# Windowed attention and a gated feed-forward layer: the last two batches' attention outputs with queries on partitions, turned through DRAM

## The chip, the cores and the metric

The kernel runs on one core of a Trainium2 chip. The metric is the device time of one execution in microseconds; lower is better. A core has a matrix engine (PE), a vector engine (DVE), a scalar engine (ACT), GpSimd (POOL), and a sync engine (SP) whose work here is to issue DMA transfers. SPq stands for the queue of instructions of that sync engine.

## The reference

```python
B, H, S, D = 4, 8, 768, 64           # n_sink = 4, window = 128
scores = q @ k.T / sqrt(D)           # per batch and head
keep = (pos_k < 4) | ((0 <= pos_q - pos_k) & (pos_q - pos_k < 128))
a = exp(scores) where keep, divided by its sum over the keys
x = (a @ v), heads side by side      # (B*S, 512)
out = (relu(x @ w_gate) * (x @ w_val)) @ w_out   # 512 -> 1536 -> 512
```

Each query sees the first four keys and the 128 keys up to its own. The output has 3072 rows of 512 float32 values.

## The kernel before

**Units.** A unit is one pair of heads of one batch: four units a batch (`NP`), 16 in all. Unit u of batch b is number 4b + u. Keys are cut into blocks of 128 columns of `kE`; from the second block on, a block holds the four sink keys and 124 or so keys of the window, so that a query needs two neighbouring blocks only.

**Scores.** `Sg(u, s)` multiplies key blocks (the stationary operand, 64 rows for each head, the two heads in the two row halves of the array) with the queries (the moving operand) into a pair of PSUM banks. ACT takes the exponentials into `ee` (keys on partitions, queries along the columns, in bf16), and DVE multiplies them by a mask. A unit has three score groups, s = 0, 1, 2.

**Values.** `V(u, part)` takes half of the queries (384, `CUT`). `V1` multiplies `ee` by a block of ones, which gives the sums of the exponentials in 64 rows for each head; `V3` multiplies `ee` by the values `vn`. In both, `ones` or `vn` is stationary (64 columns for each head, two heads in the two column halves) and `ee` is moving. `V2` turns the sums, takes reciprocals and turns them back (two 32x32 block transposes by DVE), and `V4` multiplies and writes `xT`, with the features of x on partitions, as the feed-forward layer needs it.

**Feed-forward.** `chunk(b, g, m)` makes 128 of the 1536 hidden features for 384 tokens: four matmuls with `wg`, four with `wv`, a relu by ACT, a product by DVE into `hT`. It reads `xT` of all four units of the batch. `ffn2` is the second matrix product, twelve matmuls for 128 tokens, then a copy by ACT to `ot` and a store by SP.

**The order.** Nothing is reordered by a scheduler: each engine does its instructions in program order. The loop near the end runs over 96 slots, one chunk each: 24 slots a batch, 12 for the first half of the tokens (g = 0), 12 for the second. In a slot come first the things in `prep[s]` (loads, casts, transfers), then the chunk, then what `plan[s]` lists (scores and values of units to come), then three matmuls of `ffn2`. Batch 0 is done ahead of the loop and in its first slots; batch b's attention runs while batch b - 1 is in the feed-forward layer. With a `w` string of pairs, the kernel before puts two items (V or S) into every second slot.

**Keys and queries of batches 2 and 3** (units 8 to 15, `ND` = 8) come another way: `to_dram` (on POOL) writes them in bf16 to DRAM tensors `kd` and `qd`, `turn` (on SP) reads them back with five transposing DMAs, four into `kE` and one into `qT`, and `sinks` copies the four sink columns. When each happens follows from the plan:

```python
t = at["S", i - NP, 2] + 1        # the slot after the last scores of the unit with the same buffers
prep[t - 6].append(("td", i))     # to_dram
prep[t].append(("turn", i))
prep[at["S", i, 0] - 1].append(("sinks", i))
```

The values of a batch are loaded to `vf` by 13 DMAs on SP (`load_v`), seven slots ahead of the first V, and cast to `vn` by POOL in seven blocks (`cast_v`), some three slots ahead.

**Buffers.** Two pairs of PSUM banks `PP` take scores, values and sums in turn; three banks `G` serve the chunks, the fourth `ffn2`. There are two `xT`, two `hT`, two `vn`, four `ee`, four `kE` and `qT`, three `ot`.

Of the kernel before, what the change touches and what calls it, by code (L numbers as in the profile page):

```python
# [9 lines left out]
F32 = mybir.dt.float32  # L10
BF16 = mybir.dt.bfloat16
Alu = mybir.AluOpType
# [7 lines left out]
def kernel(  # L20
# [12 lines left out]
    nc = tc.nc  # L33
    B, H, S, D = q.shape
    assert (B, H, S, D) == (4, 8, 768, 64)
    NP = H // 2
# [14 lines left out]
    kf = [const.tile([128, S], F32, name=f"kf{i}") for i in range(NQ)]  # L51
    qf = [const.tile([128, S], F32, name=f"qf{i}") for i in range(NQ)]
    vf = const.tile([128, 7, H, 64], F32, name="vf")
    vn = [const.tile([128, 7, H, 64], BF16, name=f"vn{i}") for i in range(2)]
    qT = [const.tile([128, S], BF16, name=f"qT{i}") for i in range(NT)]
    kE = [const.tile([128, 896], BF16, name=f"kE{i}") for i in range(NT)]
    ee = [const.tile([128, 3, 2, 512], BF16, name=f"ee{i}") for i in range(NE)]
    qn = [const.tile([128, S], BF16, name=f"qn{i}") for i in range(2)]
    kn = [const.tile([128, S], BF16, name=f"kn{i}") for i in range(2)]
    wg = const.tile([128, KO, d_ff], BF16, name="wg")  # L60
# [27 lines left out]
            [(2, 1, 140, 255, 0), (3, 1, 267, 507, 0)] + VLAST]  # L88
    VSEG0 = [[(0, 0, 0, 247, 0), (1, 0, 247, 499, 120), (2, 1, 0, 140, 244), (3, 1, 140, 152, 372)],
             [(2, 1, 152, 267, 0), (3, 1, 267, 507, 0)] + VLAST]  # L90

    class Unit:
        def __init__(self, i):
# [33 lines left out]
                nc.sync.dma_start(out=vf[a0:a1, j, :, :], in_=v[b, :, s0:s0 + a1 - a0, :].rearrange("h s d -> s h d"))  # L127

    def cast_v(b, j, rows=128, copy=nc.gpsimd.tensor_copy):
        flat = lambda ap: ap.rearrange("p h d -> p (h d)")  # L130
        copy(flat(vn[b % 2][0:rows, j, :, :]), flat(vf[0:rows, j, :, :]))  # L131

    def cast_kq(u):
        for src, dst in ((kf[u.i % NQ], kn[u.i % 2]), (qf[u.i % NQ], qn[u.i % 2])):
# [2 lines left out]
    def gate(u):  # L137
# [4 lines left out]
    ND = 2 * NP  # L142
    kd, qd = ([nc.dram_tensor(f"{x}d{i}", (S, 128), BF16, kind="Internal").ap() for i in range(ND, B * NP)]
              for x in "kq")

    def to_dram(u):
        for x, dst in ((k, kd), (q, qd)):
            nc.gpsimd.dma_start(out=dst[u.i - ND].rearrange("s (h d) -> s h d", h=2),  # L148
                                in_=x[u.b, 2 * u.p:2 * u.p + 2].rearrange("h s d -> s h d"))
# [21 lines left out]
    def setup():  # L171
        nc.vector.memset(warm[:], 0.0)
        nc.scalar.activation(warm[:], warm[:], Act.Exp, bias=0.0, scale=1.0)
        make_identity(nc, ident)

        nc.gpsimd.memset(band[:], 1.0)
        nc.gpsimd.affine_select(out=band[:], in_=band[:], compare_op=Alu.is_ge, fill=0.0, base=0,
                                pattern=[[1, 256]], channel_multiplier=-1)
        nc.gpsimd.affine_select(out=band[:], in_=band[:], compare_op=Alu.is_ge, fill=0.0, base=127,
                                pattern=[[-1, 256]], channel_multiplier=1)  # L180
        nc.gpsimd.affine_select(out=msk[:, 0, 0:247], in_=band[:, 0:247], compare_op=Alu.is_ge, fill=0.0,
                                base=119, pattern=[[0, 247]], channel_multiplier=-1)
        cp, ms = nc.vector.tensor_copy, nc.vector.memset
        for i in range(NT):
            ms(kE[i][:, 120:124], 0.0)
            ms(kE[i][:, 396:508], 0.0)
            ms(kE[i][:, 784:896], 0.0)
        ms(ones[:], 1.0)
        ms(vn[0][:, 3, :, :], 0.0)
        ms(vf[:, 6, :, :], 0.0)  # L190
        cp(msk[:, 0, 247:499], band[:, 4:256])
        ms(msk[0:4, 0, 247:499], 1.0)
        ms(msk[0:4, 0, 0:120], 1.0)
        ms(msk[0:4, 0, 120:247], 0.0)
        bias(mb[:, 0, 0:499], msk[:, 0, 0:499])
        bias(mb[:, 1, 0:140], band[:, 0:140])
        bias(mb[:, 1, 140:152], band[:, 4:16])
        ms(mb[0:4, 1, 140:152], 0.0)
# [16 lines left out]
    def pair():  # L215
        rot[0] += 1
        return PP[rot[0] % 2]
# [76 lines left out]
    def sums(u, part, out, w):  # L294
        segs = (VSEG if u.b else VSEG0)[part]
        for i, (j, g, c0, c1, o0) in enumerate(segs):
            for h in range(2):
                nc.tensor.matmul(out=out[64 * h:64 * h + 64, o0:o0 + c1 - c0], lhsT=w(j, h),  # L298
                                 rhs=ee[u.i % NE][:, g, h, c0:c1], start=i == 0, stop=i == len(segs) - 1,
                                 skip_group_check=True)  # L300
# [7 lines left out]
    def V2(u, part, pv, pd):  # L308

        t1 = npool.tile([128, CUT], F32, name="t1")  # L310
        R = npool.tile([128, CUT], F32, name="R")
        r = npool.tile([128, CUT // 32], F32, name="r")
        nc.vector.transpose(out=t1[:], in_=pd[:, 0:CUT])  # L313
        nc.vector.reciprocal(r[:], t1[:].rearrange("p (c e) -> p c e", e=32)[:, :, 0])
        nc.vector.transpose(out=R[:].rearrange("p (c e) -> p c e", e=32),  # L315
                            in_=r[:].unsqueeze(2).to_broadcast([128, CUT // 32, 32]))
        return u, part, pv, R

    def V3(u, part, pv):
        sums(u, part, pv, lambda j, h: vn[u.b % 2][:, j, 2 * u.p + h, :])  # L320

    def V4(u, part, pv, R):
        nc.vector.tensor_tensor(xT[u.b % 2][:, u.p, CUT * part:CUT * part + CUT], pv[:, 0:CUT], R[:], op=Alu.mult)  # L323
        ready[u.b, u.p, part] = True

    def V(u, part):
        x = V1(u, part)
        V3(*x[:3])
        V4(*V2(*x))

    gvn = [0]

# [34 lines left out]
    with tc.manual_schedule():  # L367
# [65 lines left out]
        def put(s, y, n):  # L433
            st = (y[0], n * NP + int(y[1]), int(y[2]) if len(y) > 2 else 0)
            at[st] = s
            plan[s].append(st)
# [5 lines left out]
        for s, w in {12: "T0", 13: "T1", 14: "S00 S01", 15: "S10 S11", 16: "T2", 17: "S20 S21", 18: "V00",  # L442
                     19: "V10 T3", 20: "V20", 21: "S30 S31", 22: "V30 S02"}.items():
            for y in w.split():
                put(s, y, 1)
        for b in range(2, B + 1):
            if b < B:
                w = ("Vp01 Sp12 Vp11 Sp22 Vp21 Sp32 Vp31 Sn00 Sn01 Sn10 "
                     "Vn00 Sn11 Sn20 Vn10 Sn21 Sn30 Vn20 Sn31 Vn30 Sn02")
            else:  # L450
                w = "Vp01 Sp12 Vp11 Sp22 Vp21 Sp32 Vp31"
            for x, y in enumerate(w.split()):
                put(24 * (b - 1) + x // 2 * 2, y[0] + y[2:], b - (y[1] == "p"))
        prep = [[] for _ in slots]
        prep[1] += [("half", 6), ("half", 7), ("v", 0, 3), ("v", 0, 4), ("w", 6, 8), ("v", 0, 5), ("v", 0, 6),
                    ("w", 8, 10), ("w", 10, 12)]
# [1 line left out]
        prep[10] += [("kq", 4), ("load", 7), ("kq", 5)]  # L458
        prep[13] += [("kq", 6)]
        prep[15] += [("v", 1, j) for j in range(7)]  # L460
        prep[16] += [("kq", 7), ("td", 8), ("wo",)]
        for i in range(ND, len(U)):
            t = at["S", i - NP, 2] + 1
            if i > ND:
                prep[t - 6].append(("td", i))
            prep[t].append(("turn", i))
            prep[at["S", i, 0] - 1].append(("sinks", i))
            assert t < at["S", i, 0] - 2
        for b in range(2, B):
            s0 = at["V", b * NP, 0]  # L470
            prep[s0 - 7].append(("lv", b))
            for j in range(7):
                prep[s0 - 3 + j // 2 if j < 6 else s0].append(("v", b, j))

        f2 = deque()
        for s, (b, g, m) in enumerate(slots):
            for x in prep[s]:
                if x[0] == "kq":
                    cast_kq(U[x[1]])
                elif x[0] == "load":  # L480
                    gate(U[x[1]])
                    load_kq(U[x[1]])
                elif x[0] == "half":
                    cast_half(x[1])
                elif x[0] == "w":
                    load_w(*x[1:])
                elif x[0] == "wo":
                    for c in range(3):
                        load_wo(c)
                elif x[0] == "td":  # L490
                    to_dram(U[x[1]])
                elif x[0] == "turn":
                    turn(U[x[1]])
                elif x[0] == "sinks":
                    sinks(U[x[1]], nc.gpsimd.tensor_copy)
                elif x[0] == "lv":
                    for j in range(7):
                        load_v(x[1], j)
                else:
                    cast_v(*x[1:])  # L500
            chunk(b, g, m)
            for what, i, x in plan[s]:
                if what == "T":
                    T(U[i])
                elif what == "H":
                    T_half(NP + i)
                elif what == "S":
                    Sg(U[i], x)
                else:
                    V(U[i], x)  # L510
            for _ in range(3):
                if f2:
                    f2.popleft()()
            if s == 23:
                f2 += [lambda t=t, mm=mm: ffn2(0, t, mm) for t in range(6) for mm in range(FM)]
            if b > 0 and m == FM - 1:
                f2 += [lambda b=b, t=t, mm=mm: ffn2(b, t, mm) for t in range(3 * g, 3 * g + 3) for mm in range(FM)]
# [38 lines left out]
```

The softmax here doesn't subtract the row's maximum and nothing guards it: scores larger than these inputs give would overflow.

## Time and profile before

| what | value |
|---|---|
| time, median of 3 runs | 263.45 us (263.05 to 265.11) |
| span of the profiled execution | 261.9 us |
| PE busy | 247.7 us, 95% of the span |
| DVE, ACT, POOL busy | 151.2, 116.5, 73.0 us |
| share of the 16 DMA engines, hardware queue of SP | 34.3% |
| start of slots 24, 34 and 48 (first chunk matmul, L340) | 75.12, 100.29 and 133.43 us |
| start of the last slot, 95 | 240.34 us |
| chain of waits, the largest shares | L360 20%, L340 19%, L345 19%, L298 (pp) 7% |

In the profile, L340 and L345 are the first product of the feed-forward layer, L360 the second, L282 the scores, L298 the sums and values (`ones` and `vn`), L286 the exponentials, L289 the masks, L313 to L323 the normalization, L154 and L155 the transposing DMAs of `turn`, L127 the loads of v, L148 the transfers of `to_dram`, L131 the casts of v. A row of the timeline has the start and duration in microseconds, the engine, the line, the operation, the result and operands with their form, the number of instructions merged into the row, and in brackets what the engine waited for. A form such as 128\*64 says how many rows and columns of the PE array an instruction uses.

### The profile page before, as it was taken

The numbers are of one execution on the slowest core, as the hardware profiler recorded it, in microseconds if no ns is written. First come the engines' busy times: TensorE is split into PE (matmuls) and PEld (weight loads), VectorE is DVE, ScalarE is ACT, GpSimd is POOL, SyncE is SP. The second block draws the span as 40 slices with busy tenths as digits, with TensorE's granted clock in tenths as the row PEclk, the third lists the DMA queues.
The fourth block names the chain that finished last, engine by engine and source line by source line (L and its number), as shares of the span: only waits on it lengthen the run. The fifth ranks groups of instructions, "written<-read, shape, count | busy, mean of one in ns | idle before, by whom it ended". The sixth has DMA issues, their size and how long they took to land.

```text
span 261.9 us, 5490 instructions
## 1 busy us (share of the span) xinstructions
PE 247.7 (95%) x2143; PEld 140.5 (54%) x2143; DVE 151.2 (58%) x316; ACT 116.5 (44%) x224; POOL 73.0 (28%) x100
## 2 busy tenths in 40 slices
PE   7877899998899999999999999999999999999994
PEld 2454565655555555555555555555555655555441
DVE  7675888487987665657357567667265742323000
ACT  3765742594543454454333464463344233332211
POOL 6791631759960003894000033000000000000000
PEclk9999999999999999999999999999999999999998
DMA  7999997995999969499712393310110011101232
GB/s 192 275 248 191 149 131 194 309 238 56 158 170 155 115 133 203 98 163 145 117 52 62 69 219 85 109 43 0 40 43 7 36 40 40 41 4 40 80 123 80
DMA packets 81266, 30.45 MB, mean 116 GB/s; under 512 B 65368, under 2 KB 77144, under 8 KB 81240
## 3 DMA queue, kind: packets, MB, share of 16 engines
q1 hardware_dynamic: 47944, 21.83, 34.3%
q0 software_dynamic: 32752, 7.87, 34.1%
q8 instruction: 17, 0.28, 0.5%
q10 hardware_dynamic: 544, 0.39, 0.5%
q14 instruction: 9, 0.07, 0.1%
HBM read 28.48 MB, written 9.44 MB: 145 GB/s over the span
## 4 chain that ended last, share of the span: by engine, by line
PE 74%; DMA 8%; DVE 7%; ACT 3%; issue 3%; SPq 2%; POOL 1%; DVEq 0%; ACTq 0%
PE g L360 20%; PE g L340 19%; PE g L345 19%; PE pp L298 7%; DMA vf<-in_v_dram 5%; PE pp L360 4%; PE pp L282 4%; DMA wv<-in_moe_w_val_dram 3%; ACT ee L286 3%; SPq L127 2%; DVE hT L347 2%; DVE t L313 1%; DVE R L315 1%; DVE ee L289 1%; DVE qT L246 1%
## 5 line engine op out<-in xcount | busy, mean ns | idle before, releaser
L347 DVE TENSOR_TENSOR hT<-gs,g 128x384 bf16<-128x384 f32 x96 | 52.8, 550 | 65.5 <-PE g L345 64.7
L340 PE MATMUL g<-xT,wg 128*128 128x384 bf16 x384 | 78.4, 326 | 0.7 <-DVE hT L347 0.5
L345 PE MATMUL g<-xT,wv 128*128 128x384 bf16 x384 | 78.1, 326 | 0.7 <-DMA wv<-in_moe_w_val_dram 0.7
L343 ACT ACTIVATE gs<-g 128x384 f32<-128x384 f32 x96 | 47.4, 494 | 69.1 <-PE g L340 67.2
L360 PE MATMUL g<-wo,hT 128*128 128x512 bf16 x240 | 64.1, 380 | 0.0
L286 ACT ACTIVATE ee<-pp 128x998 bf16<-128x998 f32 (+4 forms) x52 | 45.3, 902 | 34.9 <-PE pp L282 34.8
L340 PEld LDWEIGHTS <-wg 128*128 128x128 bf16 x384 | 36.0, 98 | 32.5 <-issue 2.1
L345 PEld LDWEIGHTS <-wv 128*128 128x128 bf16 x384 | 37.5, 98 | 26.0 <-DMA wv<-in_moe_w_val_dram 1.1
L360 PEld LDWEIGHTS <-hT 128*128 128x128 bf16 x288 | 26.2, 98 | 26.2 <-issue 2.1
L289 DVE TENSOR_TENSOR ee<-ee,msk 128x838 bf16<-128x838 bf16 (+4 forms) x48 | 30.0, 633 | 10.7 <-ACT ee L286 10.6
L131 POOL CAST vn<-vf 128x512 bf16<-128x512 f32 x28 | 18.1, 654 | 39.7 <-DMA vf<-in_v_dram 37.3
L148 POOL DMA_DIRECT2D qd<-in_q_dram x8 | 25.1, 4452 | 0.0
L148 POOL DMA_DIRECT2D kd<-in_k_dram x8 | 22.7, 3910 | 0.3 <-issue 0.3
L282 PE MATMUL pp<-qT,kE 64*128 64x255 bf16 (+6 forms) x240 | 17.2, 246 | 3.7 <-DVE qT L267 1.7
L364 ACT COPY ot<-g 128x512 f32<-128x512 f32 x20 | 11.7, 586 | 18.2 <-PE g L360 17.4
L315 DVE STREAM_TRANSPOSE R<-r 128x384 f32<-128x384 f32 x32 | 18.5, 578 | 1.1
L313 DVE STREAM_TRANSPOSE t<-pp 128x384 f32<-128x384 f32 x28 | 16.2, 580 | 4.1 <-PE pp L298 3.5
L298 PEld LDWEIGHTS <-ones 128*64 128x64 bf16 x288 | 12.6, 109 | 10.4 <-issue 9.8
L323 DVE TENSOR_TENSOR xT<-pp,R 128x384 bf16<-128x384 f32 x28 | 15.6, 557 | 1.0
L282 PEld LDWEIGHTS <-kE 64*128 64x128 bf16 x240 | 8.8, 94 | 11.8 <-issue 8.4
L298 PE MATMUL pp<-ee,ones 128*64 128x115 bf16 (+8 forms) x256 | 14.4, 237 | 0.2
L298 PE MATMUL pp<-ee,vn 128*64 128x115 bf16 (+8 forms) x256 | 13.9, 233 | 0.5 <-POOL vn L131 0.5
(74 smaller groups left out, 129.3 us busy)
## 6 DMA issues: line engine op xcount, KB each, us to landing
out_dram<-ot SPq DMA_DIRECT2D x24, 256.0 KB
vf<-in_v_dram SPq DMA_DIRECT2D x12, 256.0 KB
vf<-in_v_dram SPq DMA_DIRECT2D x12, 224.0 KB
kf<-in_k_dram SPq DMA_DIRECT2D x8, 192.0 KB
wg<-in_moe_w_gate_dram POOLq DMA_DIRECT2D x6, 256.0 KB, 7.2
wv<-in_moe_w_val_dram POOLq DMA_DIRECT2D x6, 256.0 KB, 8.1
kf<-in_k_dram SPq DMA_DIRECT2D x4, 384.0 KB
qf<-in_q_dram SPq DMA_DIRECT2D x4, 384.0 KB
```

The lines of the kernel that those rows point to most:

```text
L148: nc.gpsimd.dma_start(out=dst[u.i - ND].rearrange("s (h d) -> s h d", h=2), in_=x[u.b, 2 * u.p:2 * u.p + 2].rearrange("h s d -> s h d"))
L282: nc.tensor.matmul(out=ps[:, h, c0:c1], lhsT=kE[t][64 * h:64 * h + 64, x0:x0 + 128], rhs=qT[t][64 * h:64 * h + 64, q0:q0 + c1 - c0], start ...
L286: nc.scalar.activation(x, ps[:, :, b0:n], Act.Exp, bias=0.0, scale=scale)
L289: nc.vector.tensor_tensor(x, x, msk[:, g, m0:m0 + c1 - c0].unsqueeze(1).to_broadcast([128, 2, c1 - c0]), op=Alu.mult)
L298: nc.tensor.matmul(out=out[64 * h:64 * h + 64, o0:o0 + c1 - c0], lhsT=w(j, h), rhs=ee[u.i % NE][:, g, h, c0:c1], start=i == 0, stop=i == l ...
L313: nc.vector.transpose(out=t1[:], in_=pd[:, 0:CUT])
L315: nc.vector.transpose(out=R[:].rearrange("p (c e) -> p c e", e=32), in_=r[:].unsqueeze(2).to_broadcast([128, CUT // 32, 32]))
L340: nc.tensor.matmul(out=gp[:, 0:CUT], lhsT=wg[:, ko, m * 128:(m + 1) * 128], rhs=x[:, ko, c], start=ko == 0, stop=ko == KO - 1)
L343: nc.scalar.activation(gs[:], gp[:, 0:CUT], Act.Relu, bias=0.0, scale=1.0)
L345: nc.tensor.matmul(out=vp[:, 0:CUT], lhsT=wv[:, ko, m * 128:(m + 1) * 128], rhs=x[:, ko, c], start=ko == 0, stop=ko == KO - 1)
L347: nc.vector.tensor_tensor(h[:, m, c], gs[:], vp[:, 0:CUT], op=Alu.mult)
L360: nc.tensor.matmul(out=op, lhsT=hT[b % 2][:, m, t * 128:(t + 1) * 128], rhs=wo[:, m, :], start=m == 0, stop=m == FM - 1)
```

## The change

For batches 2 and 3, `V1` to `V4` give way to `W(u)`. The exponentials `ee` become the stationary operand, up to 128 queries at a time, and the values move, 64 columns with a 65th column of ones beside them. The result has queries on partitions and, in its 65th column, the sum of the exponentials: no second pass with `ones`, and no turning of the sums, since the reciprocal is now one number for each partition. There are seven tiles of queries (`QSEG`); where a key block begins inside a tile, a small extra matmul with 3 or 20 query columns adds what is missing.

The output then has the wrong side on partitions for the feed-forward layer. DVE writes it to `xn` in bf16; `x_to_dram` stores it in DRAM with four DMAs, and two slots later `x_turn` reads it back with one transposing DMA of 768 rows into `xT`. Both are issued by SP.

The plan is rewritten for these batches: scores come in pairs in one slot, and W once for each unit. Batch 2's W stand in slots 34, 36, 40 and 42, batch 3's in 53, 55, 60 and 62. Since the times of `turn` and `to_dram` follow from the plan, those of units 12 to 15 come earlier than before.

```diff
-    vn = [const.tile([128, 7, H, 64], BF16, name=f"vn{i}") for i in range(2)]
+    vn = [const.tile([128, 7, H, 66], BF16, name=f"vn{i}") for i in range(2)]
+    xn = [const.tile([128, 7, 128], BF16, name=f"xn{i}") for i in range(2)]
+    rn = [const.tile([128, 2, 7], F32, name=f"rn{i}") for i in range(2)]
+    QSEG = [[(0, 0, 0, 128)], [(0, 0, 120, 128), (1, 0, 247, 128)],
+            [(1, 0, 371, 128), (2, 1, 0, 128), (0, 0, 244, 3)], [(2, 1, 128, 128), (3, 1, 255, 128)],
+            [(3, 1, 379, 128), (4, 2, 0, 128), (2, 1, 252, 3)], [(4, 2, 128, 128), (5, 2, 255, 128)],
+            [(5, 2, 379, 128), (6, 2, 399, 20), (4, 2, 252, 3)]]
...
+    def x_to_dram(u):
+        x, d = xn[u.i % 2], xd[u.i - ND]
+        nc.sync.dma_start(out=d[0:120, :], in_=x[0:120, 0, :])
+        for t, r0, n, i in ((1, 120, 124, 3), (2, 244, 128, 2)):
+            nc.sync.dma_start(out=d[r0:r0 + 252 * i, :].rearrange("(i r) c -> r i c", r=252)[0:n, :, :],
+                              in_=x[0:n, t:t + 2 * i - 1:2, :])
+        nc.sync.dma_start(out=d[748:768, :], in_=x[0:20, 6, :])
+
+    def x_turn(u):
+        nc.sync.dma_start(out=xT[u.b % 2][:, u.p, :], in_=xd[u.i - ND][0:S, :], transpose=True)
...
+    def setup3():
+        for i in range(2):
+            nc.gpsimd.memset(vn[i][:, :, :, 64:66], 1.0)
+        for i in range(NE):
+            nc.gpsimd.memset(ee[i][:, 2, :, 419:512], 1.0)
+
+    def W(u):
+        ps = pair()
+        for h in range(2):
+            for t, segs in enumerate(QSEG):
+                for i, (j, g, c0, n) in enumerate(segs):
+                    nc.tensor.matmul(out=ps[0:n, h, 65 * t:65 * t + 65], lhsT=ee[u.i % NE][:, g, h, c0:c0 + n],
+                                     rhs=vn[u.b % 2][:, j, 2 * u.p + h, 0:65], start=t == 0 and i == 0,
+                                     stop=t == 6 and i == len(segs) - 1, skip_group_check=True)
+        o = ps[:, :, 0:455].rearrange("p h (t e) -> p h t e", e=65)
+        x, r = xn[u.i % 2], rn[u.i % 2]
+        nc.vector.reciprocal(r[:], o[:, :, :, 64])
+        nc.vector.tensor_tensor(x[:].rearrange("p t (h d) -> p h t d", h=2), o[:, :, :, 0:64],
+                                r[:].unsqueeze(3).to_broadcast([128, 2, 7, 64]), op=Alu.mult)
+        x_to_dram(u)
...
-        for b in range(2, B + 1):
-            if b < B:
-                w = ("Vp01 Sp12 Vp11 Sp22 Vp21 Sp32 Vp31 Sn00 Sn01 Sn10 "
-                     "Vn00 Sn11 Sn20 Vn10 Sn21 Sn30 Vn20 Sn31 Vn30 Sn02")
-            else:
-                w = "Vp01 Sp12 Vp11 Sp22 Vp21 Sp32 Vp31"
-            for x, y in enumerate(w.split()):
-                put(24 * (b - 1) + x // 2 * 2, y[0] + y[2:], b - (y[1] == "p"))
+        for s, w in {24: "V01 S12", 26: "V11 S22", 28: "V21 S32", 30: "V31"}.items():
+            for y in w.split():
+                put(s, y, 1)
+        for b, sl in ((2, {29: "S00 S01", 31: "S02 S10", 33: "S11 S12", 34: "W0", 35: "S20 S21", 36: "W1",
+                           37: "S22 S30", 39: "S31 S32", 40: "W2", 42: "W3"}),
+                      (3, {48: "S00 S01", 50: "S02 S10", 52: "S11 S12", 53: "W0", 54: "S20 S21", 55: "W1",
+                           57: "S22 S30", 59: "S31 S32", 60: "W2", 62: "W3"})):
+            for s, w in sl.items():
+                for y in w.split():
+                    put(s, y, b)
...
+        prep[14] += [("setup3",)]
...
+            prep[at["W", i, 0] + 2].append(("xturn", i))
         for b in range(2, B):
-            s0 = at["V", b * NP, 0]
+            s0 = at["W", b * NP, 0]
             prep[s0 - 7].append(("lv", b))
```

More of the change, by code (lines that the diff above doesn't have):

```diff
@@ L129, in cast_v @@
     def cast_v(b, j, rows=128, copy=nc.gpsimd.tensor_copy):
-        flat = lambda ap: ap.rearrange("p h d -> p (h d)")
-        copy(flat(vn[b % 2][0:rows, j, :, :]), flat(vf[0:rows, j, :, :]))
+        copy(vn[b % 2][0:rows, j, :, 0:64], vf[0:rows, j, :, :])
     def cast_kq(u):
@@ L144 @@
               for x in "kq")
+    xd = [nc.dram_tensor(f"xd{i}", (S + 128, 128), BF16, kind="Internal").ap() for i in range(ND, B * NP)]
+    def x_to_dram(u):
[7 more added lines that the diff above has]
+        nc.sync.dma_start(out=xT[u.b % 2][:, u.p, :], in_=xd[u.i - ND][0:S, :], transpose=True)
+        for x in range(2):
+            ready[u.b, u.p, x] = True
     def to_dram(u):
@@ L188, in setup @@
         ms(ones[:], 1.0)
-        ms(vn[0][:, 3, :, :], 0.0)
+        ms(vn[0][:, 3, :, 0:64], 0.0)
         ms(vf[:, 6, :, :], 0.0)
@@ L319, in V3 @@
     def V3(u, part, pv):
-        sums(u, part, pv, lambda j, h: vn[u.b % 2][:, j, 2 * u.p + h, :])
+        sums(u, part, pv, lambda j, h: vn[u.b % 2][:, j, 2 * u.p + h, 0:64])
     def V4(u, part, pv, R):
@@ L491 @@
                     to_dram(U[x[1]])
+                elif x[0] == "setup3":
+                    setup3()
+                elif x[0] == "xturn":
+                    x_turn(U[x[1]])
                 elif x[0] == "turn":
@@ L508 @@
                     Sg(U[i], x)
+                elif what == "W":
+                    W(U[i])
                 else:
```

## The prediction

> **What bounds the kernel now.** First the busy shares, then the PE timeline of a stretch of the steady stage, then the timelines of the sync engine's queue (SPq) and of PE at the places that the change touches.
>
> ```profile
> PE 247.7 (95%) x2143; PEld 140.5 (54%) x2143; DVE 151.2 (58%) x316; ACT 116.5 (44%) x224; POOL 73.0 (28%) x100
> ```
>
> PE is the bound, but a busy PE is not a streaming PE, so the starts must be read (start, duration, engine, line, operation):
>
> ```profile
> 130.19 0.81 PE L345 MATMUL g<-xT,wv 128*128 128x384 bf16 x4
> 130.84 0.81 PE L360 MATMUL g<-wo,hT 128*128 128x512 bf16 x3
> 131.48 0.81 PE L340 MATMUL g<-xT,wg 128*128 128x384 bf16 x4
> ...
> 134.82 0.53 PE L298 MATMUL pp<-ee,ones 128*64 128x115 bf16 x10
> 135.21 0.51 PE L298 MATMUL pp<-ee,vn 128*64 128x115 bf16 x10
> 135.66 0.36 PE L282 MATMUL pp<-qT,kE 64*128 64x255 bf16 x6
> 135.94 0.82 PE L360 MATMUL g<-wo,hT 128*128 128x512 bf16 x3
> ```
>
> Four matmuls of 384 columns take 0.65 us (130.19 to 130.84): 2.36 columns per ns, nothing lost. A slot without attention is 0.65 + 0.65 + 0.65 = 1.95 us. The score group (L282) streams pairs of 255, 144 and 20 columns side by side, 419 columns or 0.18 us, yet takes 0.28 (135.66 to 135.94). The trace's matmul starts show the same hole, 91 to 98 ns, at every change of the tile form (128\*128, 128\*64, 64\*128); within a form there is none. I price a change of form at 0.105 us with the first weight load behind it. V of part 1 takes 0.84 us (134.82 to 135.66), of part 0 0.72.
>
> The other resource is SPq, which issues in program order and holds everything behind an instruction that waits:
>
> ```profile
> 80.16 5.21 SPq L154 DMA_TRANSPOSE kE<-kd  x4
> 85.47 2.02 SPq L155 DMA_TRANSPOSE qT<-qd  x1
> 87.59 5.02 SPq L154 DMA_TRANSPOSE kE<-kd  x4
> 92.72 1.22 SPq L155 DMA_TRANSPOSE qT<-qd  x1
> 94.03 7.67 SPq L127 DMA_DIRECT2D vf<-in_v_dram  x13
> 101.80 0.38 SPq L365 DMA_DIRECT2D out_dram<-ot  x1
> 102.27 4.96 SPq L154 DMA_TRANSPOSE kE<-kd  x4
> 107.33 1.22 SPq L155 DMA_TRANSPOSE qT<-qd  x1
> ```
>
> From 80 to 108.6 us SPq has no gap. One turn of a unit (five transposes) takes 6.3 us and up to 7.4, about 1.2 for each transpose. It costs that in a quiet stretch too:
>
> ```profile
> 134.68 4.95 SPq L154 DMA_TRANSPOSE kE<-kd  x4
> 139.72 1.23 SPq L155 DMA_TRANSPOSE qT<-qd  x1
> 141.05 5.01 SPq L154 DMA_TRANSPOSE kE<-kd  x4
> 146.16 2.32 SPq L155 DMA_TRANSPOSE qT<-qd  x1
> ```
>
> So it is the issue, not DMA traffic. The stores behind it wait for it too: slot 27's store, ready at about 86, is issued at 101.80. And the values of batch 2 already come just too late for PE:
>
> ```profile
> 102.95 0.20 PE L298 MATMUL pp<-ee,vn 128*64 128x12 bf16 x2 [0.49 <-POOL vn L131]
> ```
>
> **What the Trainium skill says.** "DMA: Bandwidth & Descriptors", section "Two DMAs through the same engine are not ordered": a DMA that reads what another wrote has to wait, on the issuing engine, for the first one's completion. SPq's waits for kd in the trace before (9.6 us at the longest) are of this kind. Same page, "Why a DMA increments its semaphore by 16 and not by 1": a DMA uses the largest count of engines up to 16 that divides the slowest dimension; for the new copy of 124 x 3 rows that is 4. No run here shows a 124. "TensorE: Matmul & The Clock Gate", Part 1: after an idle window of about 3.4 us the PE clock halves, and needs about as long to recover. The trace agrees at the start only: the idle-tile matmuls of 512 columns average 496 ns against 380 later.
>
> **The change, part by part.**
>
> *PE, attention times values.* Per unit V0 and V1 go, 0.72 + 0.84 = 1.56 us. W has 32 matmuls of 65 columns: 24 with a 128-column weight tile, 8 with 3 or 20 columns, which the built program gives the form 128\*32. Streaming is 65 / 2.36 = 28 ns, say 30. The weight load could bind: six transposes (L260) with full 128-column loads and 128 moving columns run from 22.67 to 23.01, 57 ns each, so it costs at most that. I take 30, since T's pairs of 64-column loads (L238) already go at 32 to 37 ns; bound 57. The 8 narrow ones stand apart, so the form changes 12 times. W = 32 x 0.030 + 12 x 0.105 = 2.2 us; low 1.2, if 128\*32 to 128\*128 is free; high 2.9, with 57 ns. That is 0.6 per unit more than V, partly repaid because the scores now come in pairs (0.62 us a pair) and share their form changes.
>
> *DVE.* Two transposes, a reciprocal and a product in each half (580 + 228 + 578 + 557 ns, 3.9 us a unit) become a reciprocal of 14 and one product of 896 elements, 0.25 + at most 557 x 896/384 = 1.55 us. DVE is at 58%, so nothing of this saving lies on the path; I only use that x stands in xn 1.5 us after W. setup3 and the wider vn cost PE nothing: early POOL memsets and the same casts.
>
> *POOL.* Units 13 to 15 now convert k and q among batch 2's value casts. In the queue order, unit 14 precedes value block 2 and unit 15 block 6. Each is two issues of 0.87 us (L148 starts at 107.90, 108.77). The last cast, ended at 106.4 before, ends at about 108.1; W0 of batch 2, which needs all blocks, could start at 102.5, and ends at about 109.4.
>
> *SPq, the part that decides.* The built program's SPq order after the load of v for batch 2 is: turn 11; store; turn 12; turn 13; x to DRAM 8; store; x turn 8; x to DRAM 9; x turn 9; turn 14; store; turn 15; x to DRAM 10; x turn 10; x to DRAM 11; store; x turn 11. Each x turn waits there until its four copies have landed. Turns 14 and 15 serve batch 3 but stand ahead of x of units 10 and 11, which slot 48 needs. Costs: turn 6.35 (6.9 for one of the four); store 0.4; four copies 1.9 to issue; the 124 x 3 one, issued 0.5 in, has 93 rows on each of 4 engines. Packets of 256 bytes took 18 to 31 ns, of 128 bytes written to DRAM about 35: 1.7 to 3.3 us, and 1.35 fixed (the output store at 134.24 landed at 136.25, with 0.67 for its eight packets of 84 ns on each engine). So a unit's x lands 3.5 to 5.2 after it starts, I take 4.3. A transpose of 768 rows issues in 1.2 to 2.3 (1.7) and lands 2.65 to 3.9 after its start (3.2; the semaphores of the ones at 139.72 and 146.16).
>
> Ledger: turn 11 ends 108.55; store 109.0; turns 12 and 13 121.7; x 8 lands 126.0, its turn issued 127.7; x 9 132.0, 133.7; turn 14, store, turn 15 147.4; x 10 151.7, 153.4; x 11 157.7, turned 160.9. Low ends sum to 155, high to 169.
>
> *PE up to slot 48.* Slots 24 to 33 take 26.1 (25.2 before), W0's slot ends at 110.1; 13 x 1.95 + three pairs of scores 1.9 + three W 6.6 gives slot 48 at 144. Its chunk reads xT of all four units, the last 0.5 us in, so it starts at 160.4: PE, in order, stands for 16 us. Nothing can hide this, for scores and ffn2 stand behind the chunk.
>
> *From slot 48.* To slot 95: 47 x 1.95 = 91.6, six pairs of scores 3.7, four W 8.8. From there to the end as before, 261.9 - 240.3 = 21.5. Halved clock after the wait, an estimate by the clock page: 3.4 us at half speed, 1.7 lost. No second wait: batch 3's W end by slot 62, ten slots ahead of their use, with no turns in the queue. Sum 160.4 + 91.6 + 3.7 + 8.8 + 21.5 + 1.7 = 287.7; plus 1.6 between span and measured time (263.45 - 261.9): 289.3.
>
> **The rivals.**
> - *Only PE's own work counts.* If issues overlap more than I read, so that x is there in time, slot 48 starts at 144: 144 + 91.6 + 3.7 + 8.8 + 21.5 + 1.6 = 271.2. For it: the copies are small and the DMA engines are mostly idle from 109 us on. Against it: the sums of issue times alone, with no landing waited for, reach 150.
> - *A faster kernel.* W with free form changes (1.2), values in time, x in time: slot 48 at 101.2 + 14 x 1.95 + 1.9 + 4 x 1.2 = 135.2, the end at 135.2 + 91.6 + 3.7 + 4.8 + 21.5 + 1.6 = 258.4. For it: fewer columns and less DVE work. It needs SPq to be no limit as well.
> - *More queueing.* Copies slower than 35 ns a row, or the late v load of batch 3 holding W of slot 53: some 15 us more, 304.
>
> **How the numbers follow.** My forecast 0.80, PE alone 0.10, faster 0.06, more queueing 0.04. Time 289.3. Ledger (-5.5, +8.5), W (-4, +2.8) and clock (-1.7, +1.5) would reach 278 to 302 if all fell together; 279 to 300 leaves out little of it, with the rivals under 2 in 10. Faster 0.07, same 0.02, slower 0.91.
>
> **What would show it.** Right: a PE gap of 10 to 22 us ahead of slot 48 that ends on a DMA of xT; SPq without idle time from 102 to about 158 except for waits on xd; x turns 10 and 11 behind turn 15; W near 2.2 us with twelve holes of 0.1; a wait for POOL's vn at W0; the PE clock lower after the gap. Wrong: slot 48 reached at 144 or before without a wait, turns that issue in well under 6 us, or a W of about 1 us without holes.

## The result, and the profile after

The changed kernel takes **290.54 us** (median of 4 runs, 289.31 to 292.19); the kernel before took 264.28 beside it (263.05 to 265.22). The ratio is 1.1001, 95% interval 1.0919 to 1.1082: slower by a tenth. The forecast was 289.3, with a range of 279 to 300. Here and below, ratios leave out runs in a slower state that some executions show, medians keep them.

From the page of the kernel after, taken in the slowest of its four runs (292.19): busy time, PE and its granted clock in 40 slices, the chain's shares by engine, and two groups (line, engine, form, count; busy us, mean ns; idle ahead and what ended it).

```profile
PE 255.5 (88%) x2087; PEld 144.2 (50%) x2111; DVE 133.5 (46%) x268; ACT 114.4 (39%) x224; POOL 74.5 (26%) x106
PE   7778799997999954999990599999999999999994
PEclk9999999999999985799998599999999999999999
PE 68%; DMA 10%; DVE 7%; issue 4%; POOL 4%; SPq 3%; ACT 3%; POOLq 0%; DVEq 0%; ACTq 0%
L386 PE MATMUL g<-xT,wg 128*128 128x384 bf16 x384 | 80.3, 331 | 10.7 <-DMA xT<-xd 9.9
L367 PE MATMUL pp<-vn,ee 128*128 128x65 bf16 (+2 forms) x256 | 19.4, 199 | 7.6 <-POOL vn L139 7.6
```

PE was busy for 95% of the span and is now for 88%. Two holes stand out in its row (the "54" and the "05"), each with a dip of the clock. The idle columns name them: 9.9 us for xT to come back from DRAM, 7.6 us for the casts of v. (L386, L391 and L406 are now the products with wg, wv and wo; L306 the scores; L367 W; L178 and L179 the turns of keys and queries; L159 to L163 the copies of x; L166 its turn; L172 the conversions; L139 the casts.)

Taken from the first chunk matmul of each slot, the span divides so (us):

| stretch | before | after | last run of the study, e12_gaps |
|---|---|---|---|
| up to slot 24 | 75.12 | 76.44 | 76.39 |
| slots 24 to 33 | 25.17 | 26.34 | 26.33 |
| slot 34 | 3.78 | **13.92** | 3.11 |
| slots 35 to 47 | 29.36 | 35.44 | 31.39 |
| slot 48 | 3.17 | **14.81** | 2.94 |
| slots 49 to 94 | 103.74 | 102.00 | 104.70 |
| slot 95 to the end | 21.54 | 21.54 | 21.54 |

The first row is no effect: with identical work up to there, changed kernels reached slot 24 between 74.8 and 77.0. Slots 34 and 48 hold 21.8 of the 28.6 us between the spans. Another 6.1 in slots 35 to 47 is work: 1.75 from the low clock in slot 35, the rest mostly W and the scores that used to stand after slot 48.

**Slot 48.** The PE timeline of the kernel after:

```profile
152.13 0.49 PE L386 MATMUL g<-xT,wg 128*128 128x384 bf16 x2
158.00 0.48 PE L386 MATMUL g<-xT,wg 128*128 128x384 bf16 x1 [5.37 <-DMA xT<-xd]
163.05 0.48 PE L386 MATMUL g<-xT,wg 128*128 128x384 bf16 x1 [4.57 <-DMA xT<-xd]
```

The first two pairs of heads are there; the third and the fourth are waited for one after the other. The queue that brings them, SPq's timeline of the same kernel:

```profile
119.17 4.95 SPq L178 DMA_TRANSPOSE kE<-kd  x4
124.21 1.98 SPq L179 DMA_TRANSPOSE qT<-qd  x1
126.29 0.54 SPq L159 DMA_DIRECT2D xd<-xn  x1
...
130.12 1.15 SPq L166 DMA_TRANSPOSE xT<-xd  x1
131.36 0.53 SPq L159 DMA_DIRECT2D xd<-xn  x1
...
135.78 1.15 SPq L166 DMA_TRANSPOSE xT<-xd  x1
137.04 6.00 SPq L178 DMA_TRANSPOSE kE<-kd  x4
143.09 1.27 SPq L179 DMA_TRANSPOSE qT<-qd  x1
144.40 0.58 SPq L411 DMA_DIRECT2D out_dram<-ot  x1
145.09 4.95 SPq L178 DMA_TRANSPOSE kE<-kd  x4
150.13 1.23 SPq L179 DMA_TRANSPOSE qT<-qd  x1
151.45 0.54 SPq L159 DMA_DIRECT2D xd<-xn  x1
...
155.11 1.15 SPq L166 DMA_TRANSPOSE xT<-xd  x1
156.36 0.53 SPq L159 DMA_DIRECT2D xd<-xn  x1
...
160.19 1.15 SPq L166 DMA_TRANSPOSE xT<-xd  x1
```

The order is the forecast one. Turns 14 and 15 fill 137.04 to 151.36; x of units 10 and 11 stands behind them. The last x turn starts at 160.19, and PE goes on 2.86 us later.

**Slot 34.** POOL's timeline of the kernel after:

```profile
104.20 1.61 POOL L172 DMA_DIRECT2D kd<-in_k_dram  x1
105.08 2.38 POOL L172 DMA_DIRECT2D qd<-in_q_dram  x1
105.95 3.77 POOL L139 CAST vn<-vf 128x512 bf16<-128x512 f32 x4
108.61 1.24 POOL L183 COPY kE<-kE 128x12 bf16<-128x12 bf16 x1
108.75 2.68 POOL L172 DMA_DIRECT2D kd<-in_k_dram  x1
109.62 3.45 POOL L172 DMA_DIRECT2D qd<-in_q_dram  x1
110.49 3.19 POOL L139 CAST vn<-vf 128x512 bf16<-128x512 f32 x1
```

Rows overlap here, so their ends must be read. The two DMAs of unit 14's conversion end at 105.81 and 107.46, 1.65 apart, though they start 0.88 apart; only then do the four casts run, to 109.72. Unit 15's end at 111.43 and 113.07, and the last cast at 113.68. PE, in its timeline, follows at once, and then pays once more:

```profile
108.12 0.82 PE L367 MATMUL pp<-vn,ee 128*128 128x65 bf16 x5 [3.59 <-POOL vn L139]
...
113.73 1.77 PE L367 MATMUL pp<-vn,ee 128*20 128x65 bf16 x18 [3.69 <-POOL vn L139]
...
116.69 1.49 PE L386 MATMUL g<-xT,wg 128*128 128x384 bf16 x4
```

Four matmuls of L386 take 1.28 us (116.69 to 117.97 in the next row) in place of 0.65: the halved clock.

### The profile page after: what moved, and what is told of

The parts are those of the page before. It is cut to its first block, busy times and chain, and to the rows that moved or that the text cites. A ratio compares the mean times of both kernels' runs of the same rounds, so it can differ in the third digit from the quotient of the medians.

```text
span 290.5 us, 5426 instructions
## 1 busy us (share of the span) xinstructions
PE 255.5 (88%) x2087; PEld 144.2 (50%) x2111; DVE 133.5 (46%) x268; ACT 114.4 (39%) x224; POOL 74.5 (26%) x106
## 3 DMA queue, kind: packets, MB, share of 16 engines
q0 software_dynamic: 32752, 7.87, 29.4%
## 4 chain that ended last, share of the span: by engine, by line
PE 68%; DMA 10%; DVE 7%; issue 4%; POOL 4%; SPq 3%; ACT 3%; POOLq 0%; DVEq 0%; ACTq 0%
PE g L386 18%; PE g L391 18%; PE g L406 17%; PE pp L367 6%; DMA vf<-in_v_dram 5%; PE pp L406 4%; PE pp L306 3%; DMA wv<-in_moe_w_val_dram 3%; ACT ee L310 2%; PE pp L322 2%; DVE hT L393 2%; DMA xd<-xn 1%; POOL vn L139 1%; DVE ee L313 1%; DVE t L337 1%
## 5 line engine op out<-in xcount | busy, mean ns | idle before, releaser
L389 ACT ACTIVATE gs<-g 128x384 f32<-128x384 f32 x96 | 47.6, 495 | 113.2 <-PE g L386 104.2
L386 PE MATMUL g<-xT,wg 128*128 128x384 bf16 x384 | 80.3, 331 | 10.7 <-DMA xT<-xd 9.9
L391 PE MATMUL g<-xT,wv 128*128 128x384 bf16 x384 | 79.4, 330 | 1.2 <-DMA wv<-in_moe_w_val_dram 1.2
L406 PE MATMUL g<-wo,hT 128*128 128x512 bf16 x217 | 61.3, 384 | 2.3 <-issue 1.3
L386 PEld LDWEIGHTS <-wg 128*128 128x128 bf16 x384 | 36.4, 99 | 39.1 <-issue 9.0
L391 PEld LDWEIGHTS <-wv 128*128 128x128 bf16 x384 | 37.9, 99 | 32.3 <-issue 6.5
L406 PEld LDWEIGHTS <-hT 128*128 128x128 bf16 x288 | 26.3, 98 | 27.0 <-issue 2.9
L139 POOL CAST vn<-vf 128x512 bf16<-128x512 f32 x28 | 22.7, 955 | 66.2 <-DMA vf<-in_v_dram 63.0
L367 PE MATMUL pp<-vn,ee 128*128 128x65 bf16 (+2 forms) x256 | 19.4, 199 | 7.6 <-POOL vn L139 7.6
L172 POOL DMA_DIRECT2D qd<-in_q_dram x8 | 22.3, 3191 | 0.6 <-DMA wo<-in_moe_w_out_dram 0.6
L367 PEld LDWEIGHTS <-ee 128*128 128x128 bf16 (+2 forms) x256 | 13.7, 96 | 14.0 <-issue 8.0
L306 PE MATMUL pp<-qT,kE 64*128 64x255 bf16 (+7 forms) x240 | 16.7, 254 | 4.2 <-DVE qT L291 2.4
L172 POOL DMA_DIRECT2D kd<-in_k_dram x8 | 19.1, 2920 | 0.2 <-issue 0.2
L306 PEld LDWEIGHTS <-kE 64*128 64x128 bf16 x240 | 9.3, 96 | 14.4 <-issue 11.5
L406 PE MATMUL pp<-wo,hT 128*128 128x512 bf16 x48 | 10.7, 379 | 0.0
L339 DVE STREAM_TRANSPOSE R<-r 128x384 f32<-128x384 f32 x16 | 9.3, 578 | 0.6
L322 PEld LDWEIGHTS <-ones 128*64 128x64 bf16 x144 | 6.5, 109 | 5.5 <-issue 4.9
```

The source lines that it names most:

```text
L139: copy(vn[b % 2][0:rows, j, :, 0:64], vf[0:rows, j, :, :])
L306: nc.tensor.matmul(out=ps[:, h, c0:c1], lhsT=kE[t][64 * h:64 * h + 64, x0:x0 + 128], rhs=qT[t][64 * h:64 * h + 64, q0:q0 + c1 - c0], start ...
L367: nc.tensor.matmul(out=ps[0:n, h, 65 * t:65 * t + 65], lhsT=ee[u.i % NE][:, g, h, c0:c0 + n], rhs=vn[u.b % 2][:, j, 2 * u.p + h, 0:65], st ...
L386: nc.tensor.matmul(out=gp[:, 0:CUT], lhsT=wg[:, ko, m * 128:(m + 1) * 128], rhs=x[:, ko, c], start=ko == 0, stop=ko == KO - 1)
L389: nc.scalar.activation(gs[:], gp[:, 0:CUT], Act.Relu, bias=0.0, scale=1.0)
L391: nc.tensor.matmul(out=vp[:, 0:CUT], lhsT=wv[:, ko, m * 128:(m + 1) * 128], rhs=x[:, ko, c], start=ko == 0, stop=ko == KO - 1)
```

## The experiments

Each is the kernel after with the edit that its diff shows. "Conversion 14" is `to_dram` of unit 14, two DMAs issued by POOL. From e4_narrow on, lines from W on are 3 further down in the kernels whose matmuls of W are regrouped (L370 is W, L389, L394 and L409 the three products, L414 the store).

### e1_turns: turns 14 and 15 behind the last x turn

```diff
-            prep[t].append(("turn", i))
+            if i < 14:
+                prep[t].append(("turn", i))
...
+        prep[47].append(("turn", 14))
+        prep[48].append(("turn", 15))
```

> Only the order on the sync queue is changed: the turns of units 14 and 15 (needed from slot 54 on) stand behind the x turn of unit 11, in slots 47 and 48. Queue theory: x of units 10 and 11 no longer waits behind 13 us of turns, slot 48 starts without a wait for xT, its slot falls from 14.8 to about 2.6 us, the kernel to about 278 us. Rival, the copies to DRAM and back themselves are too slow: the wait ahead of slot 48 stays, 288 to 291 us.

Measured 279.61 us; ratio to before 1.0518 [1.0444, 1.0591]. Slot 48 takes 2.59 us, without a wait, and is reached at the same time as in the kernel after (152.60). Slot 34 still takes 13.32. So it is the order in the queue, not how long copies of x take, that makes the wait of slot 48.

### e2_td: conversions 14 and 15 behind the value casts

```diff
-                prep[t - 6].append(("td", i))
+                if i < 14:
+                    prep[t - 6].append(("td", i))
...
+        prep[35] += [("td", 14), ("td", 15)]
```

> Only the DRAM conversions of k and q of units 14 and 15 on POOL are moved, behind the last value cast of batch 2 (slot 35). Queue theory: W0's wait for values in slot 34 falls from 9.8 us to 3 or 4, but slot 48 still waits for the sync queue, so the end moves by less than 1.5 us: 289 to 291. Rival, the waits add up along PE: about 282 us.

Measured 290.84 us; ratio 1.0948 [1.0865, 1.1031]: no gain. Slot 34 falls from 13.92 to 10.77, and slot 48 is reached at 146.97, 5.2 earlier. There PE waits for the same queue; its timeline:

```profile
157.23 0.48 PE L386 MATMUL g<-xT,wg 128*128 128x384 bf16 x1 [9.78 <-DMA xT<-xd]
162.16 0.48 PE L386 MATMUL g<-xT,wg 128*128 128x384 bf16 x1 [4.45 <-DMA xT<-xd]
```

The last pair arrives at 162.16, against 163.05. Two waits in a row don't add up: the earlier one only takes its time out of the later one.

### e3_both: both edits

> Both moves at once. Queue theory: PE reaches slot 48 some 8 us earlier than with the turns alone moved, there the sync queue (turns 12 and 13 ahead of x 8) holds it for about 4 us, 274 us. Waits that add up: 278 - 8 = 270 us. Copies too slow: no better than 282.

Measured 276.00 us; ratio 1.0400 [1.0327, 1.0473]. With the later wait gone, taking the earlier one away counts: 3.6 us less than e1_turns. Slot 48 is reached at 145.40 and loses 2.7. But slot 34 still takes 10.29, where 4.1 would do, though no conversion stands among the casts. PE's timeline shows why:

```profile
103.43 0.22 PE L367 MATMUL pp<-vn,ee 128*128 128x65 bf16 x2 [0.76 <-POOL vn L139]
104.67 0.45 PE L367 MATMUL pp<-vn,ee 128*128 128x65 bf16 x3 [1.02 <-POOL vn L139]
...
108.47 1.77 PE L367 MATMUL pp<-vn,ee 128*20 128x65 bf16 x18 [0.43 <-POOL vn L139]
```

W needs all seven blocks in one slot and takes them as the loads of v land. V of part 0 needed four, and part 1 came in a later slot.

### e4_narrow: in W, the 24 wide matmuls first, then the 8 narrow ones

```diff
-            for t, segs in enumerate(QSEG):
-                for i, (j, g, c0, n) in enumerate(segs):
...
+        for h, i, t, j, g, c0, n in sorted(allseg, key=lambda x: x[-1] < 128):
...
```

> The 24 wide matmuls of a W first, then its 8 narrow ones: 2 changes of tile form in place of 12, the same matmuls. Form-change theory: W falls from 2.17 to about 1.15 us; batch 2's four W lie ahead of the wait at slot 48 and give nothing, batch 3's give 4 x 1.0: about 286.5 us. Rival, the narrow matmuls are slow in themselves: W and time stay, 290 us.

Measured 287.21 us; ratio 1.0806 [1.0734, 1.0878]. PE's timeline, one whole W and what follows it, in e4_narrow and then in the kernel after:

```profile
119.77 1.22 PE L370 MATMUL pp<-vn,ee 128*128 128x65 bf16 x32
120.92 0.82 PE L409 MATMUL g<-wo,hT 128*128 128x512 bf16 x2
```

```profile
122.31 2.22 PE L367 MATMUL pp<-vn,ee 128*128 128x65 bf16 x32
124.47 0.82 PE L406 MATMUL g<-wo,hT 128*128 128x512 bf16 x2
```

From start to start W takes 1.15 us in place of 2.16. Ten changes of form less are 1.01 us, 0.10 each, with the same matmuls. Only batch 3's four W show in the end time; what batch 2 gains, slot 48 takes back (18.31 us in place of 14.81).

### e5_planv: the changed plan with V in W's slots

No W, no copies of x, no x turns: V of both halves stands where W stood.

```diff
                 elif what == "W":
-                    W(U[i])
+                    V(U[i], 0)
+                    V(U[i], 1)
...
-            prep[at["W", i, 0] + 2].append(("xturn", i))
```

> The changed plan alone: the same slots, but V of both halves in place of W, and so no copies to DRAM and no x turns. Queue theory: no wait for xT at slot 48, but the wait for values in slot 34 stays near 10 us (all seven value blocks are asked for at once, and POOL converts units 14 and 15 among the casts): about 279 us, still 5% above before. Rival, the whole loss is W's and its copies': 264 to 267 us.

Measured 276.02 us; ratio 1.0464 [1.0419, 1.0509]. Slot 34 takes 13.11, waiting for the casts as W does; slot 48 has no wait. So the plan alone, with the old arithmetic, costs some 12 us, 9.3 of them in slot 34. The way through DRAM and W are the other 15.8 us between the two spans, 12.2 of them in slot 48. The rival, that the plan would be free, falls.

### e6_pool and e7_order: a queue order meant to leave no wait

Both group the narrow matmuls, load batch 2's v and make its last cast one slot earlier, and put the conversions of batch 3 at slot 28 at the latest, ahead of the casts. e6_pool has the copies of x issued by POOL and turns 14 and 15 as in e1_turns. e7_order leaves the copies on SP, puts turns 12 to 15 behind the last x turn of batch 2, and moves batch 3's plan four slots on.

```diff
-                prep[t - 6].append(("td", i))
-            prep[t].append(("turn", i))
+                prep[min(t - 6, 28)].append(("td", i))
+            prep[{12: 45, 13: 46, 14: 51, 15: 52}.get(i, t)].append(("turn", i))
...
-            prep[s0 - 7].append(("lv", b))
+            prep[s0 - 7 - (b == 2)].append(("lv", b))
```

> The four copies of x are issued by POOL, so that the sync queue holds only the x turn; narrow matmuls grouped; v of batch 2 loaded ahead of turn 10; units 13 to 15 converted ahead of the casts; turns 14 and 15 behind x turn 11. Queue theory: neither slot 34 nor slot 48 waits; 258 to 261 us. If copies issued by POOL land some microseconds later than those of the sync queue, slot 48 waits for the difference: up to 266.

> As the last, but the copies stay on the sync queue, and turns 12 to 15 all stand behind x turn 11; batch 3's scores and W come four slots later to leave them room. Queue theory: x turn 11 lands at about 134 us, slot 48 is reached at about 136 without a wait; 258.5 us, 2% below before. If the queue is full again in batch 3, up to 265.

Measured 274.08 us, ratio 1.0377 [1.0329, 1.0426], and 273.31 us, ratio 1.0380 [1.0295, 1.0466]. Both expectations missed by some 15 us, and most of it lies in slot 34: 14.44 and 13.16. In slot 48 e6_pool still loses 1.7 (4.27 where 2.57 would do), e7_order nothing (1.95). The loads of v were early in the queue and still late. SPq's timeline of e7_order:

```profile
86.73 18.94 SPq L136 DMA_DIRECT2D vf<-in_v_dram  x13
```

Thirteen loads that took 7.67 us in the kernel before take 18.94. By POOL's timeline, six DMAs of conversions were issued from 81.74 to 89.61, and their traffic was the suspect. The view of DMA packets has it: while SP issued these loads (86.7 to 105.7), 10880 packets of POOL's DMA queue ran beside them; in the kernel before, none did.

### e8_order_wide: e7_order with W as in the change

> As the last, with the narrow matmuls where the change has them. Form-change theory: eight W longer by 1.05 us each and nothing else, 267 us, above before with no wait left. If PE has slack there: as the last.

Measured 280.81 us; ratio 1.0656 [1.0577, 1.0736]. 7.5 more than e7_order, where eight times 1.01 is 8.1: where no later wait absorbs it, the price of the form changes reaches the end.

### e9_away and e10_away_wide: the conversions away from the loads of v

Against e7_order: conversions 12 to 15 all at slot 38, batch 3's plan five slots on and turns 14 and 15 one slot later; e10_away_wide has W as in the change.

```diff
-                prep[min(t - 6, 28)].append(("td", i))
+                prep[t - 6 if i < 12 else 38].append(("td", i))
```

> As the second last (narrow matmuls grouped, turns 12 to 15 behind x turn 11), but the conversions of units 12 to 15 are moved away from the load of v, to slot 38, behind the casts; batch 3's plan five slots later. Contention theory: the 13 loads of v issue in about 8 us as before the change, not in 19; W0 in slot 34 finds its values, slot 48 starts at about 135: 258 us, 2% below before. If v is late for another reason, slot 34 still takes 13 us and the time stays near 273.

> As the last, with the narrow matmuls where the change has them. With no wait left, eight W longer by 1.05 us: 266.5 us, 1% above before. If form changes were hidden by something: as the last.

Measured 271.82 us, ratio 1.0296 [1.0254, 1.0338], and 274.03 us, ratio 1.0382 [1.0339, 1.0426]. The loads of v are back at 9.59 us and slot 34 at 3.11. But POOL now issues all eight DMAs of batch 3's conversions from 109.93 to 116.04, and the copies of x run into them. SPq's timeline of e9_away:

```profile
112.06 0.39 SPq L159 DMA_DIRECT2D xd<-xn  x1
...
120.12 1.16 SPq L166 DMA_TRANSPOSE xT<-xd  x1
121.37 0.53 SPq L159 DMA_DIRECT2D xd<-xn  x1
...
131.85 1.16 SPq L166 DMA_TRANSPOSE xT<-xd  x1
...
133.72 0.38 SPq L159 DMA_DIRECT2D xd<-xn  x1
...
137.56 1.16 SPq L166 DMA_TRANSPOSE xT<-xd  x1
```

From the first copy of a unit to its turn: 8.1 and 10.5 us, and 3.8 for the next, when the conversions are done: POOL's queue moved 12416 packets from 112 to 133 us and none from 133.7 to 138. Slot 48 loses 6.9 us. e10_away_wide loses only 2.2 us against e9_away, where its form changes would make 8.1. It reaches slot 48 just 0.6 us later, but its last x turn is issued at 140.56, not 142.54, and slot 48 takes 5.35 us in place of 8.87. Why x came earlier there isn't shown, so this pair doesn't price the form changes.

### e11_spread and e12_gaps: the conversions in other places

e11_spread has 12 to 14 early, ahead of the loads of v, and 15 at slot 52; e12_gaps has none near those loads.

```diff
-                prep[t - 6 if i < 12 else 38].append(("td", i))
+                prep[{13: 26, 14: 26, 15: 52}.get(i, t - 6)].append(("td", i))
```

and e12_gaps against e11_spread:

```diff
-                prep[{13: 26, 14: 26, 15: 52}.get(i, t - 6)].append(("td", i))
+                prep[{12: 34, 13: 37, 14: 52, 15: 52}.get(i, t - 6)].append(("td", i))
```

> As e9 (waits of the sync queue ordered, narrow matmuls grouped), but the conversions of units 12 to 14 come ahead of the load of v, right behind unit 11's, and unit 15's after the x copies, behind the sinks of unit 12: away from both the v loads and the copies of x. Contention theory: x of a unit lands within 4 us of its start again (8 and 10 us in e9 for units 8 and 9), slots 34, 37, 44 and 48 lose at most 2 us together, 260 to 262 us, 1 to 1.5% below before. If e9's long landings had another cause, slot 48 still waits and the time stays near 271.

> As the last three runs (narrow matmuls grouped, x copies on SyncE, turns 12 to 15 behind the last x turn of batch 2), with the conversions placed away from the loads of v of batch 2 (87 to 96 us), and mostly from the x copies: that of unit 12 right behind the value casts (slot 34), of unit 13 behind the sinks of unit 11 (slot 37), of units 14 and 15 behind the sinks of unit 12 (slot 52). Contention theory: the loads of v take 8 to 10 us again, slot 34 has no wait, slot 37 up to 1.2 us, slot 48 1 to 3, slot 59 up to 2: 261 to 265 us, about level with before. If the long loads of v had another cause than the traffic of the conversions, slot 34 takes about 10 us again and the time stays near 271.

e11_spread: 270.98 us, ratio 1.0272 [1.0236, 1.0309], a miss: the loads of v take 19.90 us, with 10794 packets of POOL's queue beside them, and slot 34 takes 9.63. Its copies of x, with no conversion beside them, take 3.7 to 4.5 us from the first to the turn. e12_gaps: **267.47 us**, ratio 1.0106 [1.0066, 1.0145]. Its loads of v take 7.56 us, with 38 such packets beside them, slot 34 waits for nothing, slot 48 waits 0.83: conversions beside the loads of v are what stretched them. Its time is 2.5 us above the expectation, for a reason further on. SPq and then PE in e12_gaps:

```profile
151.81 8.00 SPq L136 DMA_DIRECT2D vf<-in_v_dram  x13
...
160.48 5.93 SPq L178 DMA_TRANSPOSE kE<-kd  x4
166.50 1.23 SPq L179 DMA_TRANSPOSE qT<-qd  x1
```

```profile
162.26 0.22 PE L370 MATMUL pp<-vn,ee 128*128 128x65 bf16 x2 [0.71 <-POOL vn L139]
163.53 0.91 PE L370 MATMUL pp<-vn,ee 128*128 128x65 bf16 x22 [1.05 <-POOL vn L139]
...
169.34 1.03 PE L306 MATMUL pp<-qT,kE 64*128 64x247 bf16 x8 [2.84 <-DMA qT<-qd]
```

Turn 14 stands behind the loads of batch 3's v, and its queries are needed in slot 59. Slots 58 to 60 lose 6.5 us, slots 37 and 48 some 1.7 more. Of slots 24 to 94 that would leave 160.3 us against the 165.2 of the kernel before. That is an estimate of what the change with its narrow matmuls grouped is worth without waits, about 4.9 us; no run reached it. With the narrow matmuls where the change has them, eight W are 8.1 us longer (8 x 1.01, from e4_narrow). That makes 168.4, also an estimate: as it stands, the change would be 3.2 us slower than the kernel before even with no wait left. Whether an order exists that leaves no wait is open: the queue of SP runs from 135.90 to 174 us almost without a pause in e12_gaps, so it isn't a matter of moving one item.

## Why the prediction was right

Point by point, against the kernel after:

- **SPq decides: right.** Order, cause and place were as written, and e1_turns shows the cause by itself. PE's last wait ended at 163.05, where the ledger had x of unit 11 turned at 160.9. The sum came out close because its terms erred both ways, and that is luck. Turn 11 ended 3.4 us later than the 108.55 (the loads of v took 9.17 us from 95.91, not 7.67 from 94.03), and turn 13 4.5 later. Against that, x was in DRAM after 3.7 to 4.4 us (4.3 taken) and an x turn issued in 1.15 (1.7 taken), which left 2.2 us at the end.
- **x turned waits for its own copies: right.** The Trainium skill's "DMA: Bandwidth & Descriptors", "Two DMAs through the same engine are not ordered", asks for this wait; the chain of waits shows 2.19 us of it for unit 11. The count of engines by the same page's "Why a DMA increments its semaphore by 16 and not by 1" was right too: the copy of 124 x 3 rows sent four completion marks, one for each engine. That it lands last was wrong. Its 256-byte packets took 18 ns, and for unit 11 it landed 3.3 us after the first copy had begun; the copy of the last 20 rows, issued last, landed at 3.75.
- **POOL at W0: right in kind, wrong in size.** The step that failed is "each is two issues of 0.87 us". Each of the two DMAs holds POOL for 1.6 us: I read where rows start, and the rows of the kernel before overlapped in the same way (107.90 for 1.61 us, then 108.77 for 2.38: ends 1.64 apart). The last cast ended at 113.68, not 108.1, and slot 34 at 116.7, not 110.1. With the conversions out of the way it ended at 109.70 (e2_td), so they cost it 4.0 us where the prediction has 1.7; the rest came from the later loads of v. It didn't harm the sum, since slot 48 absorbed it: PE got there at 152.13, not 144, and waited 10 us, not 16. e2_td is the proof.
- **W: right.** 2.2 us forecast, 2.16 measured; the holes at form changes 0.10 each (e4_narrow), the narrow form no exception. The bound of 57 ns for a full weight load didn't bind: full matmuls of 65 columns started 29 to 40 ns apart. A pair of scores costs the 0.62 taken.
- **Cold clock: right in kind, too small.** By the Trainium skill's "TensorE: Matmul & The Clock Gate", Part 1, the estimate was 3.4 us at half clock and 1.7 us lost after the wait of slot 48. The granted clock was 0.50 for 5.1 us behind the last wait, and slots 48 and 49 lost about 2.4. Slot 35 lost another 1.75 (4.32 for a slot that takes 2.57 at full clock), which the sum didn't have: slot 34 also fell idle, twice for some 3.6 us.
- **DVE: right.** The product took 1.09 us and the reciprocal 0.25; DVE's busy time fell by 17.7 us and nothing of it is in the time.
- **From slot 48 on: right.** 127.4 us from the last wait (163.05) to the end, where the sum, from the same point (160.9), had 126.8. The clock makes up the difference.
- **The rivals.** PE alone (271.2) left out that W waits for v: e1_turns, without the wait of slot 48, takes 279.6. The faster kernel (258.4) needs slots 34 and 48 and those of batch 3 free of waits, which no run here had, and W at 1.2 us, which only the grouped matmuls gave (1.15).

What is behind the result, then, as far as shown: the plan alone costs some 12 us (e5_planv), since it asks for all of v in one slot and puts conversions among its casts; the order of turns ahead of x in SP's queue is worth about as much (11 us, e1_turns). They are not shares of one sum: while slot 48 waits, it absorbs what slot 34 loses (e2_td). W itself is no gain as it stands, 2.16 us against the 1.56 of the two V that it replaces, and its form changes reach the end where nothing absorbs them (7.5 us, e8_order_wide).

## What to carry to other kernels

Fewer instructions need not be less time: W has 32 matmuls where the two V have 36 (18 with `ones`, 18 with `vn`), and takes 0.6 us more. And time saved on an engine that has slack (17.7 us of DVE here) is worth nothing if it buys a longer chain through an in-order queue: write that queue out in program order, with the issue time of each item, and look for what stands ahead of the transfer that is needed first. When two waits lie in a row, mend the later one first, or both; the earlier one alone gave nothing here. And moving a transfer "to where there is room" needs a look at the traffic that runs there, not only at the queue that issues it.

## What the runs showed of the hardware

- The conversions move their rows in packets of 128 bytes, 24576 of the 32752 packets that the page counts in POOL's DMA queue. Beside 10500 to 10900 packets of that queue, 13 loads of v took 18 to 20 us of SP's queue (e6_pool, e7_order and e11_spread); beside 963 they took 9.2 (the kernel after), beside 38 they took 7.6 (e12_gaps). A unit's copies of x took 8.1 and 10.5 us beside conversions (e9_away) and 3.7 to 4.5 without (e11_spread). It shows as long rows of SP, so that it looks like a slow queue. Whether the count of packets or their bytes does it, no run separates.
- A transposing DMA costs the queue 1.1 to 1.3 us in most cases, whether it brings 768 rows of x or a block of keys; two in the kernel after, at 124.21 and 138.3, took 2.0 and 2.2. One of x lands 2.7 to 3.1 us after its start.
- Each DMA of a conversion holds POOL for 1.6 us, by the ends of its rows, though the rows start 0.87 apart.
- Each change of the PE tile form costs 0.10 us, also between the full form and the narrow one of 3 or 20 columns; grouping the narrow matmuls is worth 1.01 us in a W of 2.16.
